# Transposing x in the DMA crossbar instead of on TensorE, and casting w_in in its DMA

## Chip, cores, metric

One core of one Trainium2 chip. The metric is the device time of one execution in microseconds (us), medians of several executions. The granted clock is the part of its full clock that TensorE was given. The span is the time from the first to the last instruction of the one execution that was profiled. The chain is the work that ended last, followed back step by step to what released it. A DMA's flight goes from its issue to its landing. To evict is to copy a result out of PSUM, the memory that TensorE writes. A share of DMA time adds up the times of the packets, which overlap, so it can exceed 100% (or 1).

## The reference

A causal convolution of seven taps over the sequence, with softmaxed weights per head, and a two-layer feed-forward network with leaky ReLU.

```python
batch, seq, d_model = (8, 4096, 192); kernel_size = 7; n_heads = 8; d_ff = 2048
out = np.einsum('hk,bskhg->bshg', w, x_unf)      # conv, w = softmax(weight)
h = x @ w_in                                     # x: the conv's output, 32768 x 192
g = np.maximum(0.01 * h, h)
return (g @ w_out).astype(np.float32)
```

## The kernel before

It works through 32 blocks of 2 batches x 512 positions. The convolution runs on VectorE with channels on the partitions, so x has to be transposed. The first product (`mm1`) gives `ph`, ScalarE evicts it with the leaky ReLU to `g`, the second product (`mm2`) gives `po`. Before the first product, 40 warming matmuls, whose result nothing reads, keep TensorE busy.

```python
def transpose_x(blk):
    ts = [psum_o.tile([128, SUB, NCH, CH], BF16, name=f"ptr{i}", tag="po") for i in range(2)]
    for s in range(SUB):
        for c in range(NCH):
            for i in range(2):                       # 24 transposes, each of a 64x128 piece
                ps = slice(i * CH, (i + 1) * CH)
                nc.tensor.transpose(out=ts[i][:, s, c, :],
                    in_=x_bf[blk][ps, s, c, :, :].rearrange("p e k -> p (e k)"),
                    identity=ident[ps, ps])
    ptr[blk] = ts
# evac_x: two VectorE copies from PSUM into xt      ... (cut)

# start
load_x(0); ...; load_x(1)                            # sync queue, f32
...
cast_x(0, 0, nc.vector.tensor_copy); cast_x(0, 1, nc.scalar.copy)
transpose_x(0); evac_x(0, nc.vector.tensor_copy)
for job in conv_jobs(0): job()                       # 21 VectorE instructions
w_stage = ...                                        # w_in in f32 by sync and scalar queue
cast_x(1, 0, nc.scalar.copy); cast_x(1, 1, nc.scalar.copy)
transpose_x(1); evac_x(1, nc.scalar.copy)
for q in range(WQ): nc.scalar.copy(out=w_in[:, :, fs], in_=w_stage[:, :, fs])
...                                                  # w_out, x blocks 2 and 3 by POOL; 40 warming matmuls

# steady state, eight steps j in a block
            if blk + 2 < NBLK:
                if j == 7:
                    transpose_x(blk + 2)
                    evac_x(blk + 2, nc.vector.tensor_copy)
                    load_cast_x(blk + 4)             # cast in its DMA, by POOL
            for job in jobs[3 * j : 3 * (j + 1)]:    # conv of block blk+1
                job()
```

Of the kernel before, what the change touches and what calls it, by code (L numbers as in the profile page):

```python
# [9 lines left out]
FP32 = mybir.dt.float32  # L10
BF16 = mybir.dt.bfloat16
# [3 lines left out]
def kernel(  # L15
# [8 lines left out]
    nc = tc.nc  # L24

    B, S, D = x.shape
    H, K = weight.shape
    Din, F = moe_w_in.shape
    GRP = D // H
    HALO = 16  # L30
# [4 lines left out]
    CH = 64  # L35
    NCH = D // CH
    ST = 512
    SUB = ST // 128
    NFC = F // 128
    NB = S // ST  # L40
    NBLK = (B // 2) * NB
# [4 lines left out]
    WQ = 4  # L46

    const_pool = ctx.enter_context(tc.tile_pool(name="const", bufs=1))
    stage_pool = ctx.enter_context(tc.tile_pool(name="stage", bufs=2))
    xb_pool = ctx.enter_context(tc.tile_pool(name="xb", bufs=3))  # L50
    xt_pool = ctx.enter_context(tc.tile_pool(name="xt", bufs=2))
    yt_pool = ctx.enter_context(tc.tile_pool(name="yt", bufs=3))
    g_pool = ctx.enter_context(tc.tile_pool(name="g", bufs=3))
    o_pool = ctx.enter_context(tc.tile_pool(name="o", bufs=4))
    psum_h = ctx.enter_context(tc.tile_pool(name="ph", bufs=2, space=bass.MemoryType.PSUM))
    psum_o = ctx.enter_context(tc.tile_pool(name="po", bufs=4, space=bass.MemoryType.PSUM))
# [3 lines left out]
    out_rows = out.rearrange("(r s) d -> r s d", r=B)  # L60


    x_nat, x_bf, xt, ptr = {}, {}, {}, {}

    def load_x(blk):
        if blk >= NBLK:
            return
        rp, st = divmod(blk, NB)
        t = stage_pool.tile([128, 2, SUB, D], FP32, name="x_nat")
        for e in range(2):  # L70
            nc.sync.dma_start(  # L71
                out=t[:, e, :, :],
                in_=x[2 * rp + e, st * ST : (st + 1) * ST, :].rearrange(
                    "(c p) d -> p c d", p=128
                ),
            )
        x_nat[blk] = t

    def cast_x(blk, e, copy, half=None):
        if blk not in x_bf:  # L80
            x_bf[blk] = xb_pool.tile([128, SUB, NCH, 2, CH], BF16, name="x_bf")
        s = slice(0, SUB) if half is None else slice(half * SUB // 2, (half + 1) * SUB // 2)
        copy(  # L83
            out=x_bf[blk][:, s, :, e, :],
            in_=x_nat[blk][:, e, s, :].rearrange("p s (c k) -> p s c k", c=NCH),
        )

    def transpose_x(blk):


        ts = [psum_o.tile([128, SUB, NCH, CH], BF16, name=f"ptr{i}", tag="po") for i in range(2)]
        for s in range(SUB):
            for c in range(NCH):
                for i in range(2):
                    ps = slice(i * CH, (i + 1) * CH)
                    nc.tensor.transpose(  # L96
                        out=ts[i][:, s, c, :],
                        in_=x_bf[blk][ps, s, c, :, :].rearrange("p e k -> p (e k)"),
                        identity=ident[ps, ps],
                    )  # L100
        ptr[blk] = ts

    def evac_x(blk, copy):
        rp, st = divmod(blk, NB)
        if st == 0:
            xt[rp] = xt_pool.tile([128, NCH, HALO + S], BF16, name="xt")
            nc.vector.memset(xt[rp][:, :, 0:HALO], 0.0)
        dst = xt[rp][:, :, HALO + st * ST : HALO + (st + 1) * ST].rearrange(
            "p c (s i k) -> p i s c k", s=SUB, i=2
        )  # L110
        for i, t in enumerate(ptr.pop(blk)):
            copy(out=dst[:, i], in_=t)  # L112

    def load_cast_x(blk):

        if blk >= NBLK:
            return
        rp, st = divmod(blk, NB)
        x_bf[blk] = xb_pool.tile([128, SUB, NCH, 2, CH], BF16, name="x_bf")
        for s in range(SUB):  # L120
            for e in range(2):
                t0 = st * ST + s * 128
                nc.gpsimd.dma_start(  # L123
                    out=x_bf[blk][:, s, :, e, :],
                    in_=x[2 * rp + e, t0 : t0 + 128, :].rearrange("p (c k) -> p c k", c=NCH),
                )


    yt = {}
# [1 line left out]
    def conv_jobs(blk):  # L131
        rp, st = divmod(blk, NB)
        y = yt_pool.tile([128, NCH, ST], BF16, name="yt")
        yt[blk] = y
        jobs = []
        for c in range(NCH):
            for k in range(K):
                src = xt[rp][:, c, BASE + k + st * ST : BASE + k + (st + 1) * ST]
                dst = y[:, c, :]
                if k == 0:  # L140
                    jobs.append(
                        lambda s=src, d=dst, c=c: nc.vector.tensor_scalar_mul(  # L142
                            d, s, wk[:, c, 0:1]
                        )
                    )
                else:
                    jobs.append(
                        lambda s=src, d=dst, c=c, k=k: nc.vector.scalar_tensor_tensor(  # L148
                            out=d, in0=s, scalar=wk[:, c, k : k + 1], in1=d,
                            op0=mybir.AluOpType.mult, op1=mybir.AluOpType.add,  # L150
                        )
                    )
        return jobs


    load_x(0)
    w8 = const_pool.tile([H, K], FP32, name="w8")
    nc.scalar.dma_start(out=w8, in_=weight)
    load_x(1)

    ident = const_pool.tile([128, 128], BF16)
    make_identity(nc, ident)
# [3 lines left out]
    for sign, off in ((1, 0), (-1, GRP - 1)):  # L166
        nc.gpsimd.affine_select(
            out=sel, in_=sel, compare_op=mybir.AluOpType.is_ge, fill=0.0,
            base=off, channel_multiplier=-sign * GRP,
            pattern=[[sign * CH, NCH], [0, 2], [sign, CH]],  # L170
        )
    junk = const_pool.tile([128, 1], FP32)
    nc.vector.memset(junk, 0.0)
    nc.scalar.activation(out=junk, in_=junk, func=mybir.ActivationFunctionType.Exp)  # L174
# [5 lines left out]
        out=nmax, in_=w8, axis=mybir.AxisListType.X,  # L180
# [3 lines left out]
        out=w8, in_=w8, func=mybir.ActivationFunctionType.Exp, bias=nmax, scale=1.0,  # L184
    )
    nc.vector.tensor_reduce(
        out=ssum, in_=w8, axis=mybir.AxisListType.X, op=mybir.AluOpType.add,
# [5 lines left out]
    for c in range(NCH):  # L193
        nc.tensor.matmul(  # L194
            out=wps[:, 0, c * K : (c + 1) * K],
# [5 lines left out]
        out=wk, in_=wps[:, 0, 0 : NCH * K].rearrange("p (c k) -> p c k", c=NCH)  # L201
    )


    cast_x(0, 0, nc.vector.tensor_copy)
    cast_x(0, 1, nc.scalar.copy)
    transpose_x(0)
    evac_x(0, nc.vector.tensor_copy)
    for job in conv_jobs(0):
        job()  # L210

    w_stage = g_pool.tile([128, NCH, F], FP32, name="w_stage", tag="g")
    for q in range(WQ):
        for e in range(2):
            fs = slice(q * F // WQ, (q + 1) * F // WQ)
            (nc.sync, nc.scalar)[e].dma_start(  # L216
                out=w_stage[e * CH : (e + 1) * CH, :, fs],
                in_=moe_w_in[:, fs].rearrange("(c p) f -> p c f", p=CH),
            )

    cast_x(1, 0, nc.scalar.copy)
    cast_x(1, 1, nc.scalar.copy)
    transpose_x(1)
    evac_x(1, nc.scalar.copy)

    w_in = const_pool.tile([128, NCH, F], BF16)
    for q in range(WQ):
        fs = slice(q * F // WQ, (q + 1) * F // WQ)
        nc.scalar.copy(out=w_in[:, :, fs], in_=w_stage[:, :, fs])  # L229


    pjunk = const_pool.tile([1, 1], FP32)
    nc.gpsimd.tensor_copy(out=pjunk, in_=w_stage[0:1, NCH - 1, F - 1 : F])  # L233
    w_out = const_pool.tile([128, NFC, D], BF16)
    nc.gpsimd.dma_start(out=w_out, in_=moe_w_out.rearrange("(c p) d -> p c d", p=128))
    load_cast_x(2)
    load_cast_x(3)


    wa = psum_h.tile([128, 2, ST], FP32, name="warm", tag="ph")  # L240
    NWARM = 40
    for i in range(NWARM):
        nc.tensor.matmul(  # L243
            out=wa[:, 0, :], lhsT=ident, rhs=xt[0][:, 0, HALO : HALO + ST],
# [4 lines left out]
    g, po, osb, seal = {}, {}, {}, {}  # L249
# [75 lines left out]
    for blk in range(NBLK + 1):  # L325
        if blk < NBLK:
            g[blk] = g_pool.tile([128, NFC, 2, ST], BF16, name="g", tag="g")
        jobs = conv_jobs(blk + 1) if blk + 1 < NBLK else []
        for j in range(STEPS):
            n = (blk - 1) * STEPS + j  # L330
            if blk < NBLK:
                for f in range(FPS * j, FPS * (j + 1)):
                    act = mm1(blk, f)
                    if f == FPS * j:
                        seal[n] = act.ins.name
            if n >= 0:
                mm2(n)
            if blk + 2 < NBLK:
                if j == 7:
                    transpose_x(blk + 2)  # L340
                    evac_x(blk + 2, nc.vector.tensor_copy)
                    load_cast_x(blk + 4)
            for job in jobs[3 * j : 3 * (j + 1)]:
                job()

# [29 lines left out]
```

## Time and profile before

| | before |
|---|---|
| time, median of 4 | 720.31 us (719.12 to 722.02) |
| span of the profiled execution | 717.1 us |
| TensorE / VectorE / ScalarE / POOL busy | 98 / 79 / 71 / 26 % |
| first conv instruction of block 0 starts | 8.35 us |
| first ScalarE eviction of `ph` starts | 23.88 us |
| block period in the middle | 21.38 us |

TensorE carries the steady state and VectorE the start. The prediction quotes the lines. The time of this kernel wanders by some 3 us from one execution to the next, so small differences are read from spans within one trace.

### The profile page before, as it was taken

The page shows a single profiled execution, that of the slowest core. Times are in us where ns is not written, and L with a number is a line of the kernel's source. Part 1 is how long each engine was busy: PE and PEld are TensorE (multiplying, and loading weights), DVE is VectorE, ACT ScalarE, POOL GpSimd, SP SyncE. Part 2 cuts the span into 40 slices and gives each one's busy share as a digit, 9 for nine tenths or more (in the row PEclk, how much of TensorE's full clock was granted, in tenths as well). Part 3 has the DMA queues.
Part 4 walks back from the last instruction along what each step waited for, and adds up shares of the span by engine and source line. Part 5 has one row for each costly group of instructions (what it writes and reads, how often), then busy time and mean ns, then how long its engine had stood idle before and what let it go on. Part 6 is the DMA issues. An engine that isn't in the chain of part 4 may idle for free.

```text
span 717.1 us, 26275 instructions
## 1 busy us (share of the span) xinstructions
PE 701.7 (98%) x11933; PEld 581.9 (81%) x11934; DVE 569.3 (79%) x1002; ACT 507.5 (71%) x524; POOL 185.4 (26%) x251
## 2 busy tenths in 40 slices
PE   4899999999999999999999999999999999999998
PEld 2368888888888888888888888888888888888887
DVE  6988888888888888888888888888888888888812
ACT  3977777777777777777777777777777777777770
POOL 1853321233321233321233331133331133000000
PEclk9999999999999999999999999999999999999999
DMA  9974423444433444433444432344442344111111
GB/s 233 121 55 62 64 46 57 58 57 69 57 49 56 58 57 68 58 49 57 55 63 63 58 56 52 52 68 57 58 64 46 51 68 58 35 46 36 45 36 67
DMA packets 136782, 44.15 MB, mean 62 GB/s; under 512 B 100320, under 2 KB 135136, under 8 KB 136672
## 3 DMA queue, kind: packets, MB, share of 16 engines
q0 software_dynamic: 98064, 12.60, 27.2%
q1 hardware_dynamic: 37760, 28.32, 12.4%
q10 hardware_dynamic: 848, 1.57, 1.0%
q8 instruction: 93, 1.52, 0.9%
q14 instruction: 17, 0.14, 0.1%
HBM read 29.88 MB, written 25.17 MB: 77 GB/s over the span
## 4 chain that ended last, share of the span: by engine, by line
PE 96%; ACT 2%; DMA 1%; SPq 0%; issue 0%; ACTq 0%; DVE 0%
PE po L275 47%; PE ph L257 45%; ACT g L264 2%; PE ptr L96 2%; PE warm L243 1%; DMA x_nat<-in_x_dram 1%; ACT x_bf L83 0%; SPq L71 0%; ACTq L216 0%; DVE o_sb L317 0%
## 5 line engine op out<-in xcount | busy, mean ns | idle before, releaser
L264 ACT ACTIVATE g<-ph 128x1024 bf16<-128x1024 f32 x512 | 496.2, 1021 | 181.0 <-PE ph L257 180.9
L148 DVE SCALAR_TENSOR_TENSOR yt<-xt,wk,yt 128x512 bf16<-128x512 bf16 x576 | 431.5, 749 | 14.0
L275 PEld LDWEIGHTS <-g 64*128 64x128 bf16 (+1 forms) x8048 | 369.9, 94 | 37.4 <-issue 0.2
L275 PE MATMUL po<-w_out,g 64*128 64x192 bf16 (+1 forms) x8048 | 394.1, 243 | 0.0
L257 PE MATMUL ph<-yt,w_in 64*128 64x512 bf16 x3072 | 387.7, 376 | 2.4 <-ACT g L264 1.6
L123 POOL DMA_DIRECT2D x_bf<-in_x_dram x240 | 181.8, 763 | 400.0 <-PE ptr L96 381.4
L257 PEld LDWEIGHTS <-w_in 64*128 64x128 bf16 x3072 | 207.1, 94 | 78.2 <-issue 7.1
L317 DVE COPY o_sb<-po 128x192 f32<-128x192 f32 x256 | 91.6, 358 | 104.5 <-PE po L275 101.8
L112 DVE COPY xt<-ptr 128x768 bf16<-128x768 bf16 x62 | 31.7, 553 | 21.5 <-PE ptr L96 21.5
L142 DVE TENSOR_SCALAR yt<-xt,wk 128x512 bf16<-128x512 bf16 x96 | 35.7, 372 | 0.1
L96 PE MATMUL ptr<-ident,x_bf 64*128 64x64 bf16 x768 | 20.8, 193 | 5.2 <-ACT x_bf L83 5.2
L96 PEld LDWEIGHTS <-x_bf 64*128 64x128 bf16 x768 | 19.2, 96 | 5.8 <-ACT x_bf L83 5.4
L243 PE MATMUL warm<-xt,ident 128*128 128x512 bf16 x39 | 10.4, 429 | 0.2 <-issue 0.2
L243 PEld LDWEIGHTS <-ident 128*128 128x128 bf16 x40 | 4.3, 109 | 6.0 <-issue 2.5
L229 ACT CAST w_in<-w_stage 128x1536 bf16<-128x1536 f32 x4 | 5.8, 1472 | 4.1 <-DMA w_stage<-in_moe_w_in_dram 4.1
L83 ACT CAST x_bf<-x_nat 128x768 bf16<-128x768 f32 x3 | 2.4, 832 | 5.9 <-DMA x_nat<-in_x_dram 5.9
L194 PE MATMUL wps<-w,sel 8*128 8x7 f32 x6 | 1.4, 354 | 4.1 <-DVE w L191 4.1
L194 PEld LDWEIGHTS wps<-w,sel 8*128 8x128 f32 x6 | 1.3, 320 | 4.1 <-issue 4.1
L233 POOL COPY pjunk<-w_stage 1x1 f32<-1x1 f32 x1 | 0.2, 175 | 15.7 <-DMA w_stage<-in_moe_w_in_dram 15.7
L174 ACT ACT_TABLE_LOAD x1 | 1.3, 1283 | 1.5 <-PEq L359 1.5
L112 ACT COPY xt<-ptr 128x768 bf16<-128x768 bf16 x2 | 1.5, 802 | 0.9 <-PE ptr L96 0.9
L200 DVE COPY wk<-wps 128x21 f32<-128x21 f32 x1 | 0.2, 181 | 1.6 <-PE wps L194 1.6
(19 smaller groups left out, 5.9 us busy)
## 6 DMA issues: line engine op xcount, KB each, us to landing
out_dram<-o_sb SPq DMA_DIRECT2D x128, 192.0 KB, 2.0
x_bf<-in_x_dram POOLq DMA_DIRECT2D x240, 48.0 KB, 2.8
x_nat<-in_x_dram SPq DMA_DIRECT2D x4, 384.0 KB, 4.8
w_stage<-in_moe_w_in_dram SPq DMA_DIRECT2D x4, 384.0 KB, 10.3
w_stage<-in_moe_w_in_dram ACTq DMA_DIRECT2D x4, 384.0 KB, 13.0
w_out<-in_moe_w_out_dram POOLq DMA_DIRECT2D x1, 768.0 KB, 8.1
w<-in_weight_dram ACTq DMA_DIRECT2D x1, 0.2 KB
```

Source lines behind the costliest of these rows:

```text
L96: nc.tensor.transpose(out=ts[i][:, s, c, :], in_=x_bf[blk][ps, s, c, :, :].rearrange("p e k -> p (e k)"), identity=ident[ps, ps],)
L112: copy(out=dst[:, i], in_=t)
L123: nc.gpsimd.dma_start(out=x_bf[blk][:, s, :, e, :], in_=x[2 * rp + e, t0 : t0 + 128, :].rearrange("p (c k) -> p c k", c=NCH),)
L142: lambda s=src, d=dst, c=c: nc.vector.tensor_scalar_mul(d, s, wk[:, c, 0:1])
L148: lambda s=src, d=dst, c=c, k=k: nc.vector.scalar_tensor_tensor(out=d, in0=s, scalar=wk[:, c, k : k + 1], in1=d, op0=mybir.AluOpType.mult, ...
L194: nc.tensor.matmul(out=wps[:, 0, c * K : (c + 1) * K], lhsT=sel[:, c, :, :].rearrange("h e k -> h (e k)"), rhs=w8, start=True, stop=True,)
L229: nc.scalar.copy(out=w_in[:, :, fs], in_=w_stage[:, :, fs])
L243: nc.tensor.matmul(out=wa[:, 0, :], lhsT=ident, rhs=xt[0][:, 0, HALO : HALO + ST], start=(i == 0), stop=(i == NWARM - 1),)
L257: nc.tensor.matmul(out=ph[:, e, :], lhsT=w_in[ps, c, f * 128 : (f + 1) * 128], rhs=y[ps, c, :], start=(c == 0), stop=(c == NCH - 1),)
L264: return nc.scalar.activation(out=g[blk][:, f, :, :], in_=ph, func=mybir.ActivationFunctionType.Prelu, alpha=0.01,)
L275: ins = nc.tensor.matmul(out=po[m], lhsT=g[b][ps, fc, e, s * 128 : (s + 1) * 128], rhs=w_out[ps, fc, :], start=(rt != 1 and fc == 0), stop ...
L317: nc.vector.tensor_copy(out=o_sb[:, n % 2, :], in_=po.pop(n))
```

## The change

Intent: take the transposes off the engine that sets the pace, by letting DMAs on the sync queue do them, and the w_in casts off ScalarE.

```diff
     def transpose_x(blk):
...
-                    nc.tensor.transpose(
-                        out=ts[i][:, s, c, :],
...
+        for c in range(NCH):
+            nc.sync.dma_start_transpose(
+                out=xt[rp][:, c, HALO + st * ST : HALO + (st + 1) * ST].rearrange(
+                    "p (s k) -> p s k", s=SUB
+                ),
+                in_=t[:, c, :, :, :].rearrange("p s e k -> p (s e k)"),
+            )
...
+    w_in = const_pool.tile([128, NCH, F], BF16)      # ahead of every other DMA on POOL's queue
+    for q in range(WQ):
+        for e in range(2):
+            fs = slice(q * F // WQ, (q + 1) * F // WQ)
+            nc.gpsimd.dma_start(
+                out=w_in[e * CH : (e + 1) * CH, :, fs],
+                in_=moe_w_in[:, fs].rearrange("(c p) f -> p c f", p=CH),
+            )
...
-    evac_x(0, nc.vector.tensor_copy)
...
-    w_stage = g_pool.tile([128, NCH, F], FP32, name="w_stage", tag="g")
...
-        nc.scalar.copy(out=w_in[:, :, fs], in_=w_stage[:, :, fs])
...
-                if j == 7:
+                if j == 2:
+                    load_x(blk + 3)
+                if j == 4:
                     transpose_x(blk + 2)
-                    evac_x(blk + 2, nc.vector.tensor_copy)
-                    load_cast_x(blk + 4)
```

The x loads of the steady state become six a block, one for each channel group and batch, so that one DMA transposes a group of 128 x 512. Blocks 0 and 1 are still loaded in f32 and cast on VectorE and ScalarE.

More of the change, by code (lines that the diff above doesn't have):

```diff
@@ L60 @@
     out_rows = out.rearrange("(r s) d -> r s d", r=B)
-    x_nat, x_bf, xt, ptr = {}, {}, {}, {}
+    x_nat, x_bf, xt = {}, {}, {}
     def load_x(blk):
@@ L68, in load_x, with load_first @@
         rp, st = divmod(blk, NB)
+        t = xb_pool.tile([128, NCH, SUB, 2, CH], BF16, name="x_bf")
+        src = x[:, st * ST : (st + 1) * ST, :].rearrange("r (s p) d -> r p s d", p=128)
+        for c in range(NCH):
+            for e in range(2):
+                nc.gpsimd.dma_start(
+                    out=t[:, c, :, e, :],
+                    in_=src[2 * rp + e, :, :, c * CH : (c + 1) * CH],
+                )
+        x_bf[blk] = t
+    def load_first(blk):
         t = stage_pool.tile([128, 2, SUB, D], FP32, name="x_nat")
@@ L72, in load_x, with cast_first @@
                 out=t[:, e, :, :],
-                in_=x[2 * rp + e, st * ST : (st + 1) * ST, :].rearrange(
-                    "(c p) d -> p c d", p=128
-                ),
+                in_=x[e, blk * ST : (blk + 1) * ST, :].rearrange("(c p) d -> p c d", p=128),
             )
         x_nat[blk] = t
-    def cast_x(blk, e, copy, half=None):
-        if blk not in x_bf:
-            x_bf[blk] = xb_pool.tile([128, SUB, NCH, 2, CH], BF16, name="x_bf")
-        s = slice(0, SUB) if half is None else slice(half * SUB // 2, (half + 1) * SUB // 2)
+        x_bf[blk] = xb_pool.tile([128, NCH, SUB, 2, CH], BF16, name="x_bf")
+    def cast_first(blk, e, copy):
         copy(
-            out=x_bf[blk][:, s, :, e, :],
-            in_=x_nat[blk][:, e, s, :].rearrange("p s (c k) -> p s c k", c=NCH),
+            out=x_bf[blk][:, :, :, e, :],
+            in_=x_nat[blk][:, e, :, :].rearrange("p s (c k) -> p c s k", c=NCH),
         )
     def transpose_x(blk):
-        ts = [psum_o.tile([128, SUB, NCH, CH], BF16, name=f"ptr{i}", tag="po") for i in range(2)]
-        for s in range(SUB):
-            for c in range(NCH):
-                for i in range(2):
-                    ps = slice(i * CH, (i + 1) * CH)
-                    nc.tensor.transpose(
-                        out=ts[i][:, s, c, :],
-                        in_=x_bf[blk][ps, s, c, :, :].rearrange("p e k -> p (e k)"),
-                        identity=ident[ps, ps],
-                    )
-        ptr[blk] = ts
-    def evac_x(blk, copy):
+        if blk >= NBLK:
+            return
         rp, st = divmod(blk, NB)
@@ L107, in evac_x @@
             nc.vector.memset(xt[rp][:, :, 0:HALO], 0.0)
-        dst = xt[rp][:, :, HALO + st * ST : HALO + (st + 1) * ST].rearrange(
-            "p c (s i k) -> p i s c k", s=SUB, i=2
-        )
-        for i, t in enumerate(ptr.pop(blk)):
-            copy(out=dst[:, i], in_=t)
-    def load_cast_x(blk):
-        if blk >= NBLK:
-            return
-        rp, st = divmod(blk, NB)
-        x_bf[blk] = xb_pool.tile([128, SUB, NCH, 2, CH], BF16, name="x_bf")
-        for s in range(SUB):
-            for e in range(2):
-                t0 = st * ST + s * 128
-                nc.gpsimd.dma_start(
-                    out=x_bf[blk][:, s, :, e, :],
-                    in_=x[2 * rp + e, t0 : t0 + 128, :].rearrange("p (c k) -> p c k", c=NCH),
-                )
+        t = x_bf.pop(blk)
+        for c in range(NCH):
+            nc.sync.dma_start_transpose(
[4 more added lines that the diff above has]
+            )
     yt = {}
@@ L153, in conv_jobs @@
         return jobs
-    load_x(0)
+    load_first(0)
     w8 = const_pool.tile([H, K], FP32, name="w8")
     nc.scalar.dma_start(out=w8, in_=weight)
-    load_x(1)
+    load_first(1)
     ident = const_pool.tile([128, 128], BF16)
@@ L171 @@
         )
+    w_in = const_pool.tile([128, NCH, F], BF16)
+    for q in range(WQ):
+        for e in range(2):
+            fs = slice(q * F // WQ, (q + 1) * F // WQ)
+            nc.gpsimd.dma_start(
+                out=w_in[e * CH : (e + 1) * CH, :, fs],
+                in_=moe_w_in[:, fs].rearrange("(c p) f -> p c f", p=CH),
+            )
+    w_out = const_pool.tile([128, NFC, D], BF16)
+    nc.gpsimd.dma_start(out=w_out, in_=moe_w_out.rearrange("(c p) d -> p c d", p=128))
     junk = const_pool.tile([128, 1], FP32)
@@ L202 @@
     )
-    cast_x(0, 0, nc.vector.tensor_copy)
-    cast_x(0, 1, nc.scalar.copy)
+    cast_first(0, 0, nc.vector.tensor_copy)
+    cast_first(0, 1, nc.scalar.copy)
     transpose_x(0)
-    evac_x(0, nc.vector.tensor_copy)
     for job in conv_jobs(0):
         job()
-    w_stage = g_pool.tile([128, NCH, F], FP32, name="w_stage", tag="g")
-    for q in range(WQ):
-        for e in range(2):
-            fs = slice(q * F // WQ, (q + 1) * F // WQ)
-            (nc.sync, nc.scalar)[e].dma_start(
-                out=w_stage[e * CH : (e + 1) * CH, :, fs],
-                in_=moe_w_in[:, fs].rearrange("(c p) f -> p c f", p=CH),
-            )
-    cast_x(1, 0, nc.scalar.copy)
-    cast_x(1, 1, nc.scalar.copy)
-    transpose_x(1)
-    evac_x(1, nc.scalar.copy)
-    w_in = const_pool.tile([128, NCH, F], BF16)
-    for q in range(WQ):
-        fs = slice(q * F // WQ, (q + 1) * F // WQ)
-        nc.scalar.copy(out=w_in[:, :, fs], in_=w_stage[:, :, fs])
-    pjunk = const_pool.tile([1, 1], FP32)
-    nc.gpsimd.tensor_copy(out=pjunk, in_=w_stage[0:1, NCH - 1, F - 1 : F])
-    w_out = const_pool.tile([128, NFC, D], BF16)
-    nc.gpsimd.dma_start(out=w_out, in_=moe_w_out.rearrange("(c p) d -> p c d", p=128))
-    load_cast_x(2)
-    load_cast_x(3)
+    cast_first(1, 0, nc.scalar.copy)
+    cast_first(1, 1, nc.scalar.copy)
+    transpose_x(1)
+    load_x(2)
     wa = psum_h.tile([128, 2, ST], FP32, name="warm", tag="ph")
```

## The prediction

> **What bounds the kernel now.** I read the page's engine table first, then the chain of work that ended last, then that chain in order of time in the steady state and at the start, and last the timeline of the start.
>
> ```profile
> span 717.1 us, 26275 instructions
> PE 701.7 (98%) x11933; PEld 581.9 (81%) x11934; DVE 569.3 (79%) x1002; ACT 507.5 (71%) x524; POOL 185.4 (26%) x251
> PE 96%; ACT 2%; DMA 1%; SPq 0%; issue 0%; ACTq 0%; DVE 0%
> ...
> L123 POOL DMA_DIRECT2D x_bf<-in_x_dram x240 | 181.8, 763 | 400.0 <-PE ptr L96 381.4
> ...
> L112 DVE COPY xt<-ptr 128x768 bf16<-128x768 bf16 x62 | 31.7, 553 | 21.5 <-PE ptr L96 21.5
> ```
>
> TensorE is busy 98% of the span and is 96% of the chain. VectorE (79%) and ScalarE (71%) have slack. The row of x loads is to be read for its last field: POOL idles 400 us waiting for the PE transposes to free the buffer, so it could load earlier. The copy row is the PSUM eviction of the transposes; it costs VectorE 31.7 us, off the chain.
>
> The chain in order of time, one block in the middle and the last two blocks (start, length, what):
>
> ```profile
> 315.30 1.29 PE po L275 x32
> 316.59 0.45 PE ptr L96 x23
> 317.04 1.29 PE ph L257 x12
> ...
> 336.68 1.29 PE po L275 x32
> 337.97 0.45 PE ptr L96 x23
> 338.42 1.29 PE ph L257 x12
> ...
> 658.63 0.45 PE ptr L96 x23
> 659.07 1.30 PE ph L257 x12
> ...
> 680.03 1.30 PE ph L257 x12
> ```
>
> A block is eight steps of 12 matmuls of the first product (1.29 us) and 32 of the second (1.32). A block with transposes has a period of 338.42 - 317.04 = 21.38 us; the only one without them late in the kernel takes 680.03 - 659.07 = 20.96. So the 24 PE transposes cost the bound engine 0.42 us a block, nothing more: 24 of 64x64 stream at about 19 ns each.
>
> The start, from the timeline (start, length, engine, what):
>
> ```profile
> 5.55 0.83 ACT L83 CAST x_bf<-x_nat 128x768 bf16<-128x768 f32 x1 [2.39 <-DMA x_nat<-in_x_dram]
> 7.29 1.02 DVE L112 COPY xt<-ptr 128x768 bf16<-128x768 bf16 x2 [1.06 <-PE ptr L96]
> 8.35 0.35 DVE L142 TENSOR_SCALAR yt<-xt,wk 128x512 bf16<-128x512 bf16 x1
> ...
> 18.71 4.69 DVE L148 SCALAR_TENSOR_TENSOR yt<-xt,wk,yt 128x512 bf16<-128x512 bf16 x6
> ...
> 22.87 1.62 PE L257 MATMUL ph<-yt,w_in 64*128 64x512 bf16 x12
> 23.88 17.43 ACT L264 ACTIVATE g<-ph 128x1024 bf16<-128x1024 f32 x18
> ```
>
> The chain view charges the first 23 us to the warming matmuls and the load of x, but the timeline shows what really gates: VectorE convolves block 0 without a gap from 8.35 to 23.40 (three channel groups of 4.99 us), and the first product's accumulation needs the third group. The first ScalarE eviction at 23.88 follows. After it sixteen evictions of 0.97 us run back to back to 39.4: block 0 is ScalarE bound, so its transposes are free.
>
> **What the Trainium skill says.** "TensorE: Matmul & The Clock Gate", section Part 4: PE-mode transpose, gives about 275 ns for a 128x128 transpose in a kernel. The trace disagrees for this use: 0.45 us for the 24 is a twelfth or less of what someone would credit from 24 such transposes. "DMA: Bandwidth & Descriptors", section Latency and other measured facts, gives 261 GB/s for a crossbar transpose with a non-contiguous middle dimension, and its section Anatomy of one DMA about 2 us fixed per DMA. No transpose by DMA is in the trace of before; the fixed cost agrees with the median 2.0 us to landing of an output store and 2.8 us of an x load. The same page, Queues, rings and completion order, says that DMAs issued from one sequencer use one ring on each of the 16 DMA engines and consume descriptors in ring order. The trace of before neither shows nor contradicts it, but it matters at the start.
>
> **The change part by part.**
>
> Steady state, TensorE. Transposes are issued in blocks 0 to 29. Block 0's are hidden behind ScalarE, the other 29 go: 29 x 0.42 = 12.2 us off the path.
>
> Steady state, VectorE. A block now has 18 x 0.749 + 3 x 0.372 (conv) + 8 x 0.358 (output evictions) = 17.5 us, and loses 2 x 0.51 = 1.0 of transposed copies. It was 86% of 21.38 and becomes 83% of 20.96. It was no bound; worth 0.
>
> Steady state, x loads. 8 loads a block of 384 pieces (128 partitions x 3) become 6 of 512 (128 x 4), still 256 B read and 128 B written. The number of pieces is the same 3072, so POOL's 8 x 0.763 = 6.1 us a block and the queue's 27.2% share should stay. They start earlier, since the DMA transpose frees the buffer. Worth 0.
>
> Steady state, DMA transposes. 3 a block, each 128 x 512 bf16 = 131 kB. At the skill's 261 GB/s that is 0.5 us of moving each, my estimate from that page, plus about 2 us fixed: all landed within some 5 us of the issue. The instruction order of the changed build puts the three on the sync queue after the store of step 3 of a block. The convolution that needs them starts at step 0 of the next block: five steps x 2.62 = 13 us slack for group 0, and 6 us more for each later group (seven conv instructions, three a step). So hidden, and the queue is held for only a few us while four output buffers (eight steps, 21 us) cover the stores behind it. Worth 0.
>
> Start. Casts of block 0 end at 5.55 + 0.83 = 6.38 as before. Until now the conv started at 8.35, two us later. Now three DMA transposes go out on the sync queue at about 6.5, behind the two loads of x block 1 that the same queue issued at 1.85 and 2.39 and that landed at about 9.2. If rings are in order, the transposes move from about 9 (a little earlier, since the w_in loads leave this ring; they still compete from POOL's), and group 0 lands after its own flight, near 11. Conv starts at 11 instead of 8.35: +2.7 us. Groups 1 and 2 have 5 us of conv each to land in. The conv chain is unbroken otherwise, so the first product and ScalarE's sixteen evictions shift by the same 2.7. The warming matmuls (10.4 us) start with group 0 and end near 22, some 4 us before the last group is convolved, so TensorE may idle and start a little slow: +0.5, a guess.
>
> w_in. Four ScalarE casts of 1.47 (5.8 us) and the staging tile go. They ended at 23.8 in parallel with the conv, so once the conv ends later they are worth 0. The loads, cast on the way, are issued by POOL from about 3 us on and need to land by 26; before they landed by about 21 on two faster queues. I expect no wait.
>
> Tail. The last block, 14 us of second product alone, has no transposes: 0.
>
> Sum: 720.7 - 12.2 + 2.7 + 0.5 = 711.7; I say 712, a gain of 1.2%.
>
> **The rivals.** (a) The start costs nothing: the DMA engines interleave so that group 0 lands by 9, or VectorE's path shortens because its 1.02 us copy is gone. For it: the copy and 0.82 us of PE transposes are indeed removed. Against it: a DMA's flight of 2 us or more replaces them. Time 708 to 709. Even this stays within 2% (706.3 is the line).
> (b) The start costs much more: the transposes wait for x block 1 and share the engines with w_in's loads, at the time when the page shows the DMA nine tenths busy, or the first DMA transpose is slow to generate. Group 0 at 15 or 16 us: +7, a time of 716.
> (c) DMA transposes become the bound. If the crossbar path writes 32-byte pieces at the 32 ns a packet that the software queue shows (27.2% of 16 x 717 us over 98064 packets), one transpose is 4096 pieces or 8 us over 16 engines, three are 25 us a block, more than the 20.96 available: VectorE waits for xt, TensorE for yt, and the time goes to 780 or more. For it: nothing in the trace excludes it. Against it: the skill's bandwidth figure, and the slack of 13 us plus 6 per group, which a flight of up to 6 us each would still fit.
> (d) The traffic that is added (12.6 MB read and written in SBUF) slows the matmuls' reads. Against it: the mid-kernel step with x loads takes 2.62 us and the late one without them also 2.62. Each 1% would be 6.5 us.
>
> **Range and chances.** The gain on TensorE is measured and caps the good side: 720.7 - 12.2 = 708.5, perhaps 707 if the start gets shorter. The bad side is open: the start up to +9 us gives 718, and a partly exposed transpose more. So 707 to 722, eight in ten. Faster by over 2% needs 706.3, more than the transposes hold: 0.07. Slower by over 2% needs rival (c) or a hidden stall in each block of about 0.9 us over the gain: 0.11. The rest, 0.82, within 2%.
>
> **What would show it.** Right: no PE transposes; a block period of 20.96 in the chain; POOL's x loads near 1.0 us each; VectorE's conv of block 0 starting near 11 with a wait for a DMA transpose; the first ScalarE eviction near 26.5; output-store flight about 2 us; no wait of VectorE on a DMA in the steady state. Wrong: VectorE waiting for xt or for output buffers every block, TensorE waiting for yt, matmul steps longer than 2.62 us, or the first eviction outside 24 to 31 us.

## The result, and the profile after

714.92 us (714.71 to 715.27, 4 runs) against 720.31 (719.12 to 722.02, 4 runs). The ratio is 0.9924, 95% interval 0.9903 to 0.9945: within 2%, as forecast, 2.9 us above the predicted 712 and inside its range. Ratios here and below are those of runs of the same rounds, so not quite the ratio of the medians.

Three rows and a total of the page after (for a group: busy us, mean ns; then idle time before it and what ended most of it; for a DMA: count and us to landing):

```profile
PE 690.0 (97%) x11166; PEld 593.0 (83%) x11166; DVE 535.6 (75%) x940; ACT 500.4 (70%) x518; POOL 142.0 (20%) x198
...
L74 POOL DMA_DIRECT2D x_bf<-in_x_dram x180 | 133.6, 765 | 447.4 <-DMA xt<-x_bf 437.2
...
L127 DVE TENSOR_SCALAR yt<-xt,wk 128x512 bf16<-128x512 bf16 x96 | 33.4, 348 | 9.2 <-DMA xt<-x_bf 9.2
...
xt<-x_bf SPq DMA_TRANSPOSE x96, 2.5
```

The transposes are off TensorE. By DMA they land 2.5 us after the issue, which is the predicted 2 + 0.5. VectorE's wait for them is 9.2 us in all; the view of waits has it as one wait, so it lies at the start and nowhere else.

The chain in order of time, in the middle of the kernel after:

```profile
301.44 1.29 PE ph L230 x12
...
322.40 1.30 PE ph L230 x12
```

The period is 20.96 us, the one that a block without transposes had before.

The timeline of the start after (start, length, what, and in brackets the idle time before it):

```profile
10.85 0.83 ACT L91 CAST x_bf<-x_nat 128x768 bf16<-128x768 f32 x1 [3.15 <-DMA x_nat<-in_x_dram]
...
15.74 0.35 DVE L127 TENSOR_SCALAR yt<-xt,wk 128x512 bf16<-128x512 bf16 x1 [9.16 <-DMA xt<-x_bf]
...
30.85 1.04 PE L230 MATMUL ph<-yt,w_in 64*128 64x512 bf16 x8 [2.91 <-DVE yt L133]
31.28 1.94 ACT L237 ACTIVATE g<-ph 128x1024 bf16<-128x1024 f32 x2 [19.61 <-PE ph L230]
```

The first DMA transpose was issued at 6.64 and landed at 15.64: 9.0 us, not 2.5. The conv starts 7.4 us later than before and the first eviction too. TensorE also idles 2.91 us for the conv after its warming matmuls (and the first four matmuls of the first product), and then runs slow. The windows after show that (columns: PE, weight loads, VectorE, ScalarE and POOL busy with instruction counts; then the granted TensorE clock, the DMA share and GB/s):

```profile
28.00:32.00 4.00, 1.04 (x8) 0.43 (x8) 3.82 (x7) 0.72 (x1) 4.00 (x6) 0.99 1.79 147
32.00:36.00 4.00, 3.56 (x18) 1.32 (x18) 3.86 (x6) 3.11 (x4) 3.17 (x5) 0.59 2.00 131
```

Where the 3.8 us between the spans (717.1 and 713.3) come from, on the chains of both traces:

| part | before | after | difference |
|---|---|---|---|
| until the first eviction | 23.88 | 31.28 | +7.4 |
| sixteen evictions of block 0, to the end of the last | 15.50 | 16.50 | +1.0 |
| blocks 1 to 31 (39.42 to 699.67; 47.83 to 695.70) | 660.25 | 647.87 | -12.4 |
| the rest | 17.4 | 17.6 | +0.2 |

The medians differ by 5.4 us rather than 3.8. The profiled executions themselves took 718.91 and 715.01 us, 3.9 apart: the one of before was among its faster ones.

### The profile page after: what moved, and what is told of

It is laid out like the page before. It is cut to its first block, busy times and chain, and to the rows that moved or that the text cites. A ratio compares the mean times of both kernels' runs of the same rounds, so it can differ in the third digit from the quotient of the medians.

```text
span 713.3 us, 24704 instructions
## 1 busy us (share of the span) xinstructions
PE 690.0 (97%) x11166; PEld 593.0 (83%) x11166; DVE 535.6 (75%) x940; ACT 500.4 (70%) x518; POOL 142.0 (20%) x198
## 3 DMA queue, kind: packets, MB, share of 16 engines
q1 hardware_dynamic: 89152, 39.34, 24.0%
## 4 chain that ended last, share of the span: by engine, by line
PE 93%; DVE 2%; DMA 2%; ACT 2%; SPq 0%; issue 0%; DVEq 0%
PE po L248 48%; PE ph L230 45%; DVE yt L133 2%; ACT g L237 2%; DMA xt<-x_bf 1%; DMA x_nat<-in_x_dram 1%; SPq L83 0%; DVE yt L127 0%; DVE o_sb L290 0%; DVEq L127 0%
## 5 line engine op out<-in xcount | busy, mean ns | idle before, releaser
L248 PEld LDWEIGHTS <-g 64*128 64x128 bf16 (+1 forms) x8048 | 374.6, 94 | 32.7 <-issue 0.2
L230 PE MATMUL ph<-yt,w_in 64*128 64x512 bf16 x3072 | 393.8, 377 | 5.4 <-DVE yt L133 2.9
L248 PE MATMUL po<-w_out,g 64*128 64x192 bf16 (+1 forms) x8048 | 399.0, 243 | 0.0
L230 PEld LDWEIGHTS <-w_in 64*128 64x128 bf16 x3072 | 233.7, 94 | 62.8 <-issue 12.2
L74 POOL DMA_DIRECT2D x_bf<-in_x_dram x180 | 133.6, 765 | 447.4 <-DMA xt<-x_bf 437.2
L127 DVE TENSOR_SCALAR yt<-xt,wk 128x512 bf16<-128x512 bf16 x96 | 33.4, 348 | 9.2 <-DMA xt<-x_bf 9.2
L162 POOL DMA_DIRECT2D w_in<-in_moe_w_in_dram x8 | 5.1, 645 | 0.0
```

The source lines that it names most:

```text
L74: nc.gpsimd.dma_start(out=t[:, c, :, e, :], in_=src[2 * rp + e, :, :, c * CH : (c + 1) * CH],)
L127: lambda s=src, d=dst, c=c: nc.vector.tensor_scalar_mul(d, s, wk[:, c, 0:1])
L162: nc.gpsimd.dma_start(out=w_in[e * CH : (e + 1) * CH, :, fs], in_=moe_w_in[:, fs].rearrange("(c p) f -> p c f", p=CH),)
L230: nc.tensor.matmul(out=ph[:, e, :], lhsT=w_in[ps, c, f * 128 : (f + 1) * 128], rhs=y[ps, c, :], start=(c == 0), stop=(c == NCH - 1),)
L248: ins = nc.tensor.matmul(out=po[m], lhsT=g[b][ps, fc, e, s * 128 : (s + 1) * 128], rhs=w_out[ps, fc, :], start=(rt != 1 and fc == 0), stop ...
```

## The experiments

Theory W: the first transposes shared the DMA engines with w_in's loads, which the change moved ahead on POOL's queue. Theory Q, the one in the prediction: they wait behind x block 1 in the ring of the sync queue. Rival S: the first DMA transposes are slow to generate, whatever else runs. The table gathers what the sections below use; starts are those of the one profiled execution, and all results were correct.

| run | conv starts | first eviction | time, median | ratio to before, 95% |
|---|---|---|---|---|
| after | 15.74 | 31.28 | 714.92 | 0.9924 (0.9903 to 0.9945) |
| e1 w_in held back | 9.25 | 25.04 | 708.69 | 0.9835 (0.9820 to 0.9850) |
| e2 x block 1 later | 15.97 | 31.60 | 715.78 | 0.9935 (0.9920 to 0.9951) |
| e3 both | 9.27 | 25.00 | 709.16 | 0.9844 (0.9826 to 0.9862) |
| e4 block 0 on TensorE | 8.61 | 24.39 | 708.39 | 0.9831 (0.9815 to 0.9848) |
| e6 as e1, 60 warming | 9.26 | 24.83 | 707.90 | 0.9817 (0.9797 to 0.9838) |
| e7 w_in half alone | 8.34 | 28.32 | 719.17 | 0.9974 (0.9950 to 0.9999) |
| e8 w_in as before | 18.56 | 34.31 | 716.56 | 0.9937 (0.9911 to 0.9962) |
| e9 transposes twice | 16.49 | 32.24 | 715.14 | 0.9917 (0.9897 to 0.9937) |
| e10 four times | 16.14 | 31.89 | 715.92 | 0.9944 (0.9920 to 0.9967) |
| e11 x block 2 early | 11.60 | 27.35 | 711.74 | 0.9886 (0.9866 to 0.9907) |
| e12 as e4, 54 warming | 8.59 | 24.21 | 707.01 | 0.9820 (0.9804 to 0.9835) |

**e1, w_in held back.** The w_in, w_out and x block 2 loads follow, on POOL, a one-row copy that reads the three transposed groups of block 0.

```diff
     transpose_x(0)
+    pjunk = const_pool.tile([1, NCH], FP32)
+    nc.gpsimd.tensor_copy(out=pjunk, in_=xt[0][0:1, :, HALO])
+    # the loads of w_in and w_out stand here instead of ahead of the softmax
```

> The w_in, w_out and x block 2 loads are held back until the first three DMA transposes have landed; nothing else moves. Theory W (the transposes share the DMA engines with w_in's loads): x block 1 lands near 9 instead of 10.8, the first conv starts near 11 to 12 instead of 15.7, the first ScalarE eviction near 27 instead of 31.3, time near 711. Theory Q (ring order behind x block 1 is all): conv starts only as much earlier as x block 1 lands earlier, about 14, time 713.5. Rival S (the first transposes are slow to generate, whatever else runs): 15.7 stays, 715.

Timeline of e1:

```profile
9.25 0.35 DVE L127 TENSOR_SCALAR yt<-xt,wk 128x512 bf16<-128x512 bf16 x1 [2.65 <-DMA xt<-x_bf]
...
24.39 5.27 PE L232 MATMUL ph<-yt,w_in 64*128 64x512 bf16 x26 [4.51 <-DVE yt L133]
```

The wait falls from 9.16 to 2.65 us, about the flight of any later transpose. That is better than even theory W expected. Rival S is out: the same first instructions, with the engines free, are as fast as the rest. Theory Q as I drew it is out too: x block 1 is still ahead in the ring, but it lands before 7.9 (its second cast starts at 7.87) and holds nothing up. The DMA queues between 9.3 and 12 us show the difference, first after (packets, MB, share of 16 engines' time; q0 is POOL's queue, q1 sync's):

```profile
q0 software_dynamic: 506, 0.48, 112.6%
q1 hardware_dynamic: 146, 0.04, 15.2%
```

and e1 in the same window:

```profile
q1 hardware_dynamic: 1150, 0.28, 50.8%
```

After, w_in's kilobyte pieces fill the engines and the transposes get few packets through. In e1 they have the engines to themselves. (e1 holds back three loads together; e8 below tells w_in's apart.) Loading w_in some 9.5 us later costs nothing, since the first product waits 4.51 us for the conv anyway.

**e2, x block 1 later; e3, both.**

```diff
-    load_first(1)
...
     transpose_x(0)
+    load_first(1)
```

> The two loads of x block 1 are issued after the first three transposes instead of before them; w_in stays early. Theory Q: the transposes no longer wait on the ring, conv starts near 9.5 to 10, time near 709. Theory W: w_in still shares the engines, conv starts at 13 or later, time 712 or more. Rival S: 15.7 and 715.

> Both of the above. Theories Q and W together: the transposes run alone, conv starts at 6.6 + about 2.7 = 9.3, first eviction near 25, time near 708.5, unless w_in now lands after 25 and gates the first product. Rival S: the conv still starts at 12 or later, time 711 or more.

Timeline of e2:

```profile
15.97 0.35 DVE L127 TENSOR_SCALAR yt<-xt,wk 128x512 bf16<-128x512 bf16 x1 [9.37 <-DMA xt<-x_bf]
```

With nothing ahead of them in their ring, but w_in in flight, the transposes were as late as after: 15.97. e3 is e1 again. So the order in the ring gave nothing; the traffic from the other queue gave it all. e3's median is 0.5 us above e1's because two of its four executions took 709.9 and 710.4; they left no trace. In the profiled one (708.41) block 1's transposes land 1.5 us late for its conv, and nothing is lost: that conv ends at 40.9, and block 0's last eviction at 41.1.

**e4, block 0 on TensorE.** One part of the change undone for one block.

```diff
-    transpose_x(0)
+    transpose_pe(0, nc.vector.tensor_copy)      # 24 TensorE transposes, two copies from PSUM
```

> Only block 0 is transposed on TensorE as in the kernel before; all others by DMA. If the start alone is what the change gave back: conv starts at 8.4, first eviction at 23.9, steady state unchanged, span 713.3 - 8.4 = 705, time 706.5. If something else holds the start (w_in cast in its DMA landing late, or block 1's transposes late for the conv at 23.4), the first eviction or the end of block 0 is later than 24 and 39.5 and the time lies between 707 and 713.

The conv starts at 8.61, and 6.5 us of time come back (by medians of different rounds), not 8.4. The timeline of e4 has the missing part:

```profile
23.97 4.91 PE L251 MATMUL ph<-yt,w_in 64*128 64x512 bf16 x26 [3.24 <-DVE yt L154]
24.39 2.03 ACT L258 ACTIVATE g<-ph 128x1024 bf16<-128x1024 f32 x2 [12.24 <-PE ph L251]
```

The first eviction is 0.5 us later than before, and TensorE has again idled, 3.24 us. In the kernel before, block 1's transposes stood ahead of the warming matmuls in TensorE's order and pushed their end to 22.94; without them the warming ends before the conv does.

**e6, e1 with more warming.**

```diff
-    NWARM = 40
+    NWARM = 60
```

> The run with w_in held back, and 60 warming matmuls instead of 40. In it TensorE idled 4.5 us before the first product and the granted clock fell to 0.50 just after. If that idle time costs the 1.0 us by which the sixteen evictions of block 0 took longer than in the kernel before, they take 15.5 again, the clock stays at 1.0, and the time is about 707.6. If the longer block 0 has another cause (loads still in flight, say), it stays at 16.6 and 708.7.

The window from 24 to 28 us, in e1:

```profile
24.00:28.00 4.00, 3.61 (x18) 1.37 (x19) 3.82 (x7) 2.44 (x3) 1.52 (x2) 0.50 1.52 176
```

and in e6:

```profile
24.00:28.00 4.00, 3.25 (x26) 1.27 (x26) 3.82 (x7) 3.17 (x4) 1.67 (x3) 1.00 1.57 186
```

The clock stays at 1.00, and from the first eviction to the first matmul of the second product 16.18 us pass instead of 17.19. The loads in flight are much the same (the last two columns), so the 1.0 us of block 0 was the idle TensorE. The time moved by 0.8 (707.90 against 708.69, other rounds). The Trainium skill, "TensorE: Matmul & The Clock Gate", section Why this matters for your kernels, asks for no idle gaps over about 3 us between bursts of matmuls; the traces agree, and 2.91 us already went with it: 2.91 (after), 3.24 (e4) and 4.51 us (e1) were followed by a clock of 0.59, 0.57 and 0.50 over a 4 us window.

**e7, the w_in half alone; e8, the transposes alone.** e7 is the kernel before with w_in and w_out loaded by POOL as in the change. e8 is the changed kernel with w_in loaded, staged and cast as before.

```diff
 # e7, against before
+    (w_in, w_out loads by POOL ahead of the softmax)
-    (w_stage loads, four nc.scalar.copy, the copy that gates w_out)
 # e8, against after: the reverse, x still transposed by DMA
```

> The kernel before with the other half of the change alone: w_in cast in its DMA, every x transpose still on TensorE. The four ScalarE casts ended at 23.8, beside the first conv that ends at 23.4, so I expect the first eviction at 23.9 as before and 720, within 1 us. If w_in's casts were worth something of their own it is below 719; if the cast DMA lands late, above 721.

> The changed kernel with w_in loaded as in the kernel before: plain loads from the sync and scalar queues issued after the first transposes or from 5.6 us on, staged, cast on ScalarE. If any load beside the transposes delays them as much, conv starts near 14 to 16 and the time is 713 to 715. If it is the early cast loads from POOL that do it, the first transposes land near 10 to 11 and the time is 708.5 to 710, provided that the ScalarE casts still end before the first product.

e7 is worth 0.3% (0.0 to 0.5): its interval nearly touches 1. Its profile caught the slowest of its five executions (723.38; the others 718.99 to 719.87), so the 28.32 in the table is not typical, but it shows the same collision on another victim. The chain of that execution:

```profile
2.39 12.73 DMA x_nat<-in_x_dram
15.14 0.84 ACT x_bf L83
```

x block 1 lands at 15.1 instead of 9.2 with w_in's early loads beside it. There it holds up block 1's transposes and, behind them, the warming matmuls.

Timeline of e8:

```profile
18.56 0.35 DVE L127 TENSOR_SCALAR yt<-xt,wk 128x512 bf16<-128x512 bf16 x1 [11.95 <-DMA xt<-x_bf]
```

e8 missed both of its branches on the bad side: 716.56 us, and the conv starts at 18.56, later than with POOL's loads. But its profile, too, caught the slowest execution (718.19; the others 715.22 to 716.95), and the fastest of the four is as fast as after, so its 18.56 is not typical. So it is neither the cast nor POOL's queue that is needed: plain loads of the same weights cost about as much. Up to 11.02 these were the loads of the scalar queue alone, half of w_in's, and w_out and x block 2 went out only from 29.66. So w_in's loads suffice. The kernel before had the same loads, half of them even earlier (from 2.94), without harm; its block 0 needed no DMA after x itself.

**e9 and e10, more transposes in the steady state.**

```diff
+        if blk >= 2:
+            for i in range(1):                    # range(3) in e10
+                d = dum_pool.tile([128, NCH, ST], BF16, name="dum")
+                for c in range(NCH):
+                    nc.sync.dma_start_transpose(out=d[:, c, :]..., in_=t[:, c, :, :, :]...)
```

> From block 2 on each DMA transpose is issued twice, the second time into a tile that nothing reads (the output is right; 90 transposes more). If the transposes in the steady state are hidden, as predicted, the block period stays 20.96 and the time 715. If they are near a limit (the crossbar, the sync queue or contention with the matmuls' reads), the period grows; each 0.1 us of it is 3 us of time.

> Each DMA transpose from block 2 on is issued four times, three times into tiles that nothing reads. 12 a block x 1.22 us is 14.6 us of the sync queue's 20.96, and the output stores wait behind them. If the margin that the prediction gave (13 us before the conv needs group 0, four output buffers) is real, the period is still 20.96 and the time 715 to 717. If the queue or the crossbar gives out, VectorE waits for output buffers or for xt and the period grows by several us: 750 or more.

The sync queue (q1) on the page of after, then on that of e9:

```profile
q1 hardware_dynamic: 89152, 39.34, 24.0%
...
q1 hardware_dynamic: 138112, 51.15, 34.7%
```

The page of e10, queues and DMA issues:

```profile
q1 hardware_dynamic: 236032, 74.77, 61.3%
q0 software_dynamic: 98768, 14.17, 34.2%
...
dum<-x_bf SPq DMA_TRANSPOSE x270, 3.3
...
xt<-x_bf SPq DMA_TRANSPOSE x96, 5.8
```

and its chain in the middle:

```profile
302.09 1.29 PE ph L239 x12
...
323.04 1.29 PE ph L239 x12
```

Even with four times the transposes, packet times that add up to some 96% of the DMA engines, and the transposes that are used landing in 5.8 us, the period is 20.95. The steady state hides them with room to spare. The matmuls don't feel the traffic, which answers rival (d): one of the second product takes 243 ns on average in the kernel before, after and in e10. The count of packets also settles the prediction's rival (c): against the changed kernel's 89152 on this queue, the 270 extra transposes bring 236032 - 89152 = 146880, or 544 each, not 4096.

**e11, small pieces beside the first transposes.**

```diff
     # e1, and the six cast loads of x block 2 ahead of the softmax instead of after transpose_x(1)
```

> As the run with w_in held back until the first transposes have landed, but the six cast loads of x block 2 (3072 pieces of 128 B written) go out from POOL at about 3 us and so fly beside the first transposes. If the queues take turns packet by packet, small packets cost the transposes little: conv starts at 10 to 11, time 709 to 710. If any traffic that was queued first has to drain first, as many pieces at 32 ns over 16 engines are 6 us: conv starts at 13 or later, 712 or more.

The conv starts at 11.60, between the two branches, and the time (710.67 to 712.97, in two clusters) is at the border of the second. The profile is of the fastest execution, so 11.60 belongs to the faster cluster. Turns packet by packet, as the profile counts packets, don't fit either: between 6.7 and 9.3 us POOL's queue moved 2443 packets and the sync queue 301. What is shown is that the flight of the first transpose grows with the traffic beside it. Counted from its issue to its landing, the other queues moved:

| run | MB beside | flight, us |
|---|---|---|
| e1 | 0 | 2.5 |
| e11 | 0.39 | 4.9 |
| after | 1.37 | 9.0 |
| e2 | 1.40 | 9.2 |
| e8, slowest execution | 1.41 | 11.8 |

A longer flight also gathers more bytes, so this is no law. By what rule the engines share themselves between queues stays open.

**e12, the version to keep.** e4 with `NWARM = 54`.

> Block 0 on TensorE, all others by DMA, and 54 warming matmuls instead of 40, so that TensorE does not idle before the first product. The conv starts at 8.6, the first eviction at 24.3, block 0 takes 1.0 us less than with 40: about 707.3, the fastest version so far if so.

```profile
23.12 1.70 PE L251 MATMUL ph<-yt,w_in 64*128 64x512 bf16 x12
24.21 17.43 ACT L258 ACTIVATE g<-ph 128x1024 bf16<-128x1024 f32 x18 [12.64 <-PE ph L251]
```

No idle time before the first product, and the evictions run without a gap. 707.01 us, the lowest median here: 1.8% under the kernel before, and some 8 us under the changed one (by medians of different rounds). By the ratio to before in its own rounds e6 is as fast (0.9817 against 0.9820), so which of the two is better is not shown.

## Why the prediction was right, and where it was off

- **TensorE in the steady state, 29 x 0.42 = 12.2 us:** right. Measured 12.4, period 20.96 as the block without transposes had foretold. ("24 of 64x64" is the moving operand in the trace; the piece of x that each transposes is 64 x 128.)
- **DMA transposes hidden, about 2.5 us each, 13 us of slack:** right. Landing 2.5 us; no VectorE wait in the steady state; e9 and e10 show the slack by using it. The section that the prediction names for the fixed 2 us describes DMAs issued by GpSimd; for the sync queue, which issues the transposes, it rested on the 2.0 us of the output stores.
- **x loads "near 1.0 us each":** wrong, 0.765, as with fewer pieces before. POOL's time is per DMA here, not per piece (0.763 us with 384 pieces, 0.765 with 512), so it fell to 4.6 us a block. Off the path either way.
- **Start, "group 0 lands after its own flight, near 11 ... +2.7 us":** the mis-sized term, measured +7.4. Group 0 landed at 15.64, and the first eviction, at 31.28, fell just outside the 24 to 31 us that the prediction itself had named as a sign of being wrong. I named the competition of w_in's loads in a parenthesis and gave it nothing; rival (b), "+7", had the size and half the reason. The wait that I did price, the ring behind x block 1, gave nothing by itself (e2). Holding back w_in and the loads behind it removes 6.5 us of the wait (e1), and then group 0 lands at 9.15 and the time is 708.69, where rival (a) had put them.
- **Idle TensorE, "+0.5, a guess":** +1.0. The cause is shown by e6 for the 1.0 us of e1; the changed kernel's 1.0 has the same signs (2.91 us idle, clock 0.59).
- **The sum:** -12.2 + 2.7 + 0.5 = -9.0 predicted; -12.4 + 7.4 + 1.0 + 0.2 = -3.8 measured on the spans. By medians the gain was 5.4 us, as before's median stood 1.6 us further from its profiled span than after's. The time came within 2.9 us of 712 although the gain was missed by more than a third; the range, open to 722 for a costly start, held.
- **w_in's casts worth 0:** right within the noise (e7). The loads that came with them cost the start, but not because they were moved ahead: left as they were (e8), they cost about as much once block 0 is transposed by DMA.

## What to carry to other kernels

Work taken off the bounding engine is worth its own share of that engine's chain, read from the period with and without it, and the DMA that replaced it was free here, where there was slack. The same DMA at the start of a kernel is on the path, and there what counts is what else is in flight: order the loads by when they are needed, and hold back what can wait. After shortening or moving work ahead of a warm-up, check that TensorE still goes from it into the first matmuls without a gap.

## What the Trainium skill lacked or had wrong

- "DMA: Bandwidth & Descriptors", DMA Transpose (X-bar): no time from issue to landing for one transpose SBUF to SBUF. Here 128 x 512 bf16 (131 kB) took 1.22 us of the sync queue to issue (median) and landed in 2.5 us; it counted as 544 packets.
- The same page, Latency and other measured facts, gives 261 GB/s for the crossbar with a non-contiguous middle dimension, and "Advanced Engine Details and Errata", X-Bar Transpose (TRN2), 350 to 400. In e9 the 90 extra transposes took the queue's share from 24.0 to 34.7% of 713 us: 0.85 us of all 16 engines each, or 154 GB/s by that measure, where the packets of one transpose have the time that the profile gives them. In e1 between 9.3 and 12 us, with no other queue at work, the same measure gives about 200 GB/s (0.28 MB in 50.8% of 2.7 us). It is another measure than a rate over time, so it does not refute the pages.
- "DMA: Bandwidth & Descriptors", Rules for kernel authors, says that a transpose next to ordinary DMAs needs nothing. That holds for the results, which were correct. Of time it says nothing: ordinary loads beside it made 9.0 us of 2.5, and 11.8 us in e8's slowest execution.
- "TensorE: Matmul & The Clock Gate", Part 4: PE-mode transpose: about 275 ns for one of 128x128 in a kernel. That is the duration of one, and the page has no figure for many in a row. Here one of a 64x128 piece lasted 193 ns on average in the trace of before, but 24 in a row cost 0.42 us on the chain. So the prediction's "disagrees" sets a duration against a spacing, and another shape.
